# Thin V rows at the ends of the sequence, 128-column score weights, and other lengths in a planned kernel

## The chip, the cores and the metric

The kernel runs on one core of a Trainium2 chip. The metric is the device time of one execution in microseconds (us); the kernel before was timed three times, and the median counts. One further execution was taken with the hardware profiler, and all views of the profile are of that one.

## The reference

Two layers are applied, twice over in alternation: a segmented attention with a recurrent memory (A), and a gated feed-forward (B), each behind a layer normalisation and with a residual sum. Both applications use the same weights.

```python
x = x + A(layernorm(x))      # layer 0 attention
x = x + B(layernorm(x))
x = x + A(layernorm(x))      # layer 1 attention
x = x + B(layernorm(x))

def A(x):                    # x (1, 2048, 512); 32 heads of 128; 64 segments of 32 tokens
    mem = mem0               # 8 rows
    for s in range(64):
        h = concat([mem, x[segment s]])          # 40 rows
        q, k, v = h @ Wq, h @ Wk, h @ Wv         # per head
        p = softmax(mask(q @ k.T * scale))
        o = (p @ v) @ Wo
        mem = o[:8]; out[segment s] = o[8:]      # the memory goes to the next segment

def B(x):                    # F = 1792
    return (sigmoid(x @ w_gate) * (x @ w_up)) @ w_down
```

Data are bfloat16. The memory makes the 64 segments of a layer one after the other: no segment can begin its projections before the previous segment has finished its output projection.

## The kernel before

**Steps.** The kernel has 70 steps. In step t it works on segment t of layer 0 and on segment t - 6 of layer 1 (`LAG` = 6) together. So steps 0 to 5 hold layer 0 alone, steps 6 to 63 hold both layers, and steps 64 to 69 hold layer 1 alone. A tile hT (one of 8 in a ring) holds the normalised and transposed rows of one step in 80 columns: 32 tokens of layer 0, 8 memory rows of layer 0, 8 memory rows of layer 1, 32 tokens of layer 1. With one layer alone, 40 of the columns are used.

**Inside a step** (`emit_step`). The 32 heads go in five groups of six and one of two. For each group TensorE projects Q and K (L730, 8 matmuls of a head, weights of 128 columns from wq_sb and wk_sb, hT as the moving operand of 80 or 40 columns). ScalarE copies them to a tile qku, in which each head has 80 columns of Q followed by 80 of K. TensorE then makes the scores (L744), with the 80 columns of Q as the weights. VectorE adds the mask (L758) and does the softmax (L763 to L775) with the exponential on ScalarE (L768). TensorE transposes the probabilities (L787), and two copies bring them to ptsb. P·V follows (L808), with rows of V from a tile vsb as weights, then the output projection WO (L826), which adds up all heads in one bank. At the end the memory columns are copied to the next step's hT (L844 with one layer, L839 with two), which lets the next step begin.

**V comes in two ways.** V passes (`v_pass`, L584) take 128 token rows that were gathered in a tile (xvf or xvl) as weights, go over all 4096 columns of Wv in 32 matmuls of 512 columns, and write the result to a DRAM scratch tensor (scr). Each step reads its rows back into vsb (L685). A pass has 24 of every segment's 32 tokens. The other 8 tokens and the memory rows come from strips (`add_strips`, L698) inside the step: 32 columns of hT are the weights, four such matmuls stand side by side in the array, and 32 of them go over the 4096 columns. The result goes through a tile sst by DMA into vsb (L710).

**Which rows a pass holds.** A block is four segments (128 tokens), so 96 of its rows go through passes. For layer 0, three passes serve four blocks (`v_group`): blocks 0 to 5, 7, 8, 10, 11, 13, 14 are done this way ahead of the steps, in nine passes, of which the last (`late` = (10, 2)) is held back and planned with t = 4. Layer 1 has one pass for each block, once the block's feed-forward is done; it holds 96 rows of layer 1, and in twelve of the sixteen the other 32 rows are a third of block 6, 9, 12 or 15 of layer 0 (`v_fill`).

**Feed-forward** (`ffn`). After four segments a block has its feed-forward: two transposed products with 128 tokens moving (L926) and the down-projection (L950), with the weights streamed by GpSimd DMAs (L918, L919, L944). It uses xa for the residual sum, and the last sum of layer 1 goes to a tile xo and out. Its layer normalisations use small tiles lns, a power on GpSimd (L543) and transposes (L553).

**What sets the order.** All of this is described as tasks with a duration for each, their reads and writes, and buffers from pools. A planner (`Planner.plan`) walks through the tasks 24 times, forward and backward, with these durations, and keeps the order with the shortest span by its own account. The order on every engine and queue, and for some copies the engine too, is then fixed. So a changed duration changes the order of the whole program. Boot work carries a large `boost`: weights are loaded by SP in the order wv, then by group wq, wk and wo.

Of the kernel before, what the change touches and what calls it, by code (L numbers as in the profile page):

```python
# [16 lines left out]
P = 128  # L17
# [14 lines left out]
def mm_ns(n):  # L32
    return max(n / 2.4 + 2.3, 26.0)
# [323 lines left out]
class Kern:  # L357
# [40 lines left out]
    def setup_tiles(self):  # L398
# [10 lines left out]
        self.ident = c.tile([P, P], BF16, name="ident")  # L409
        self.maskb = c.tile([P, L], BF16, name="maskb")  # L410
        self.mask1 = c.tile([L, L], BF16, name="mask1")
        self.negh = c.tile([P, 1], F32, name="negh")
# [6 lines left out]
        self.mx = [c.tile([P, HG], F32, name=f"mx{i}") for i in range(3)]  # L419
# [5 lines left out]
        self.xo = [c.tile([P, D], BF16, name=f"xo{i}") for i in range(1)]  # L425
# [13 lines left out]
        self.lns = [c.tile([P, 12], F32, name=f"lns{i}") for i in range(3)]  # L439
# [21 lines left out]
    def clear(self):  # L461
# [3 lines left out]
        for k, t_ in enumerate(self.hT):  # L465
            pl.add("DVE", 120, lambda t_=t_: nc.vector.memset(t_[:, :, L:2 * L], 0.0), w=[("hT", k, 1, q) for q in ("m", "x")])
        for k, t_ in enumerate(self.pb):
            pl.add("DVE", 270, lambda t_=t_: nc.vector.memset(t_[:], 0.0), w=[("pb", k)])
        for k, t_ in enumerate(self.ptsb):
            pl.add("DVE", 320, lambda t_=t_: nc.vector.memset(t_[:], 0.0), w=[("ptsb", k, i) for i in (0, 1)])  # L470
        for k, t_ in enumerate(self.qku):
            pl.add("DVE", 320, lambda t_=t_: nc.vector.memset(t_[:], 0.0), w=[("qkz", k)])
        for k, t_ in enumerate(self.vsb):
            pl.add("DVE", 1130, lambda t_=t_: nc.vector.memset(t_[32:64], 0.0),
# [40 lines left out]
    def load_mem0(self):  # L515
        nc, pl, DC = self.nc, self.pl, self.DC
        m0 = self.xo[0][0:MEM, :]
        pl.add("SP", 100, lambda: nc.sync.dma_start(out=m0, in_=self.mem0), w=[("xo", 0)], lat=2500.0, boost=self.boot())
# [9 lines left out]
        pl.add("PE", 4 * 30, tr, r=[("xo", 0)], w=[B])  # L528
# [45 lines left out]
    def v_pass(self, tile, keys, pieces, boot=False):  # L574
# [3 lines left out]
        for k in range(self.H // 4):  # L578
# [15 lines left out]
            for c0, j, b, r0, n in pieces:  # L594
# [3 lines left out]
                pl.add(("SP", "POOL") if boot else "SP", {"SP": 450, "POOL": 760} if boot else 450,  # L598
# [4 lines left out]
    def v_group(self, blocks, psts, boot=False):  # L603

        cuts = [[(0, 0, 0, 24)], [(0, 96, 0, 8), (1, 0, 8, 16)], [(1, 64, 0, 16), (2, 0, 16, 8)], [(2, 32, 0, 24)]]
        base = self.cnt.get("xvf", 0)
        self.cnt["xvf"] = base + 3
        pcs = [[], [], []]
        for b, cut in zip(blocks, cuts):
            pst, B = psts[b] if b in psts else self.ln_x(b)  # L610
            for q, c0, r0, n in cut:
                xi = (base + q) % 2
                pcs[q].append((c0, 0, b, r0, n))
# [470 lines left out]
```

## Time and profile before

| what | value |
|---|---|
| median of 3 runs | 1827.25 us (1827.18 to 1829.39) |
| the profiled execution, its own time | 1827.17 us |
| its span in the trace | 1825.3 us |
| TensorE, busy | 1776.6 us |
| VectorE, ScalarE, GpSimd, busy | 1162.9, 1194.2, 569.9 us |
| moved by DMA | 272.11 MB |
| steps 0 to 5 end at | 78.4, 98.1, 116.8, 136.1, 156.2, 177.4 us |
| steps 63 to 68 end at | 1684.2, 1707.6, 1730.0, 1750.8, 1769.7, 1788.2 us |

The span is the time between the first and the last instruction of the program; the time of an execution has 1.9 us more around it. The ends of the steps are the starts of the memory copies L844 in the trace. In a group's row of the profile, the first number after the bar is the time in which at least one instruction of the group ran, and the second the mean duration of one. For TensorE a duration is not a cost: matmuls overlap in the pipeline, and what one costs is the distance between its start and that of the next. Weight loads (PEld) are rows of their own, and all of them are in the trace; of the matmuls some records are missing, so the loads serve for counting.

### The profile page before, as it was taken

What the parts mean: (1) busy time and instruction counts of PE and PEld (TensorE: products, weight loads), DVE (VectorE), ACT (ScalarE), POOL (GpSimd) and SP (SyncE); (2) the same over time, 40 slices, a digit from 0 to 9 for tenths busy, and PEclk for the clock granted to TensorE, in tenths of its full rate; (3) what the DMA queues carried; (4) which work ended last, traced back from release to release, by engine and by line L of the source; (5) the groups of instructions that cost most, each with busy time, mean ns of one, the idle gap of its engine ahead of it and who ended that gap; (6) DMA issues with size and microseconds to landing.
All of it is one profiled execution on the core that took longest, in us unless ns stands there. A gap on an engine that the chain in (4) does not pass through costs nothing.

```text
span 1825.3 us, 92117 instructions
## 1 busy us (share of the span) xinstructions
PE 1776.6 (97%) x39783; PEld 1533.6 (84%) x39970; DVE 1162.9 (64%) x3927; ACT 1194.2 (65%) x3005; POOL 569.9 (31%) x817
## 2 busy tenths in 40 slices
PE   7999999999999999999999999999999999999998
PEld 4678788988898888988898898888888898888886
DVE  5466655676666666666666667656666676656665
ACT  5666666676666666666666666666666666676664
POOL 5223032413233242413324141323324241333422
PEclk9999999999999999999999999999999999999999
DMA  9734254535445364535446363545536353544543
GB/s 351 233 108 148 62 155 121 163 100 176 147 153 157 103 204 122 170 109 169 149 124 187 109 194 100 170 131 155 158 110 196 117 168 95 173 144 127 174 124 107
DMA packets 138441, 272.11 MB, mean 149 GB/s; under 512 B 32954, under 2 KB 70594, under 8 KB 138034
## 3 DMA queue, kind: packets, MB, share of 16 engines
q0 software_dynamic: 56640, 183.09, 32.1%
q1 hardware_dynamic: 81394, 83.12, 15.4%
q8 instruction: 313, 5.13, 1.2%
q14 instruction: 94, 0.77, 0.1%
HBM read 221.85 MB, written 27.26 MB: 136 GB/s over the span
## 4 chain that ended last, share of the span: by engine, by line
PE 81%; DVE 9%; ACT 4%; SPq 3%; issue 2%; DMA 1%; POOLq 0%; ACTq 0%; DVEq 0%
PE bank L730 28%; PE bank L826 16%; PE bank L926 10%; PE bank L698 7%; PE bank L584 6%; PE bank L950 4%; PE bank L744 4%; PE bank L808 3%; DVE st L758 3%; SPq L485 3%; PE bank L787 2%; ACT ptsb L1024 1%; DVE pb L775 1%; DVE mx L763 1%; ACT qku L1024 1%
## 5 line engine op out<-in xcount | busy, mean ns | idle before, releaser
L730 PE MATMUL bank<-hT,wq_sb 128*128 128x80 bf16 (+1 forms) x8960 | 621.6, 198 | 3.5 <-issue 1.3
L730 PE MATMUL bank<-hT,wk_sb 128*128 128x80 bf16 (+1 forms) x8960 | 620.5, 198 | 3.2 <-DMA wk_sb<-in_A_Wk_dram 3.2
L1024 ACT CAST qku<-bank 128x480 bf16<-128x480 f32 (+3 forms) x770 | 391.1, 513 | 233.5 <-PE bank L730 165.7
L730 PEld LDWEIGHTS <-wq_sb 128*128 128x128 bf16 x8960 | 455.8, 99 | 38.5 <-issue 23.9
L730 PEld LDWEIGHTS <-wk_sb 128*128 128x128 bf16 x8960 | 450.6, 99 | 4.4 <-DMA wk_sb<-in_A_Wk_dram 3.6
L758 DVE TENSOR_TENSOR st<-bank,maskb 80x240 f32<-80x240 f32 (+1 forms) x732 | 267.9, 367 | 245.5 <-PE bank L744 238.7
L826 PE MATMUL bank<-otsb,wo_sb 128*128 128x80 bf16 (+1 forms) x8960 | 370.2, 198 | 9.6 <-ACT otsb L1024 8.1
L826 PEld LDWEIGHTS <-wo_sb 128*128 128x128 bf16 x8960 | 345.4, 99 | 35.0 <-issue 11.3
L918 POOL DMA_DIRECT2D wg<-in_B_w_gate_dram x217 | 164.7, 759 | 573.7 <-PE bank L926 520.2
L1024 ACT CAST otsb<-bank 128x480 bf16<-128x480 f32 (+3 forms) x420 | 199.9, 485 | 66.0 <-PE bank L808 51.7
L944 POOL DMA_DIRECT2D wd<-in_B_w_down_dram x217 | 154.2, 712 | 231.0 <-PE bank L744 88.7
L1024 ACT COPY ptsb<-bank 40x240 bf16<-40x240 bf16 (+3 forms) x546 | 170.8, 315 | 53.0 <-PE bank L787 46.0
L768 ACT ACTIVATE st<-st 80x240 f32<-80x240 f32 (+3 forms) x420 | 160.6, 383 | 45.8 <-DVE st L765 42.6
L770 DVE TENSOR_REDUCE mx<-st 80x6 f32<-80x240 f32 (+3 forms) x420 | 151.6, 364 | 50.7 <-ACT st L768 47.2
L926 PE MATMUL bank<-xnT,wg 128*128 128x128 bf16 (+2 forms) x1784 | 171.8, 218 | 2.0 <-issue 1.5
L926 PE MATMUL bank<-xnT,wu 128*128 128x128 bf16 (+2 forms) x1784 | 171.1, 218 | 0.0
L919 POOL DMA_DIRECT2D wu<-in_B_w_up_dram x217 | 162.7, 750 | 1.2 <-PE bank L926 0.5
L744 PE MATMUL bank<-qku 128*80 128x80 bf16 (+1 forms) x2240 | 160.2, 204 | 2.2 <-ACT qku L1024 1.6
L775 DVE TENSOR_TENSOR pb<-st,mx 80x240 bf16<-80x240 f32 (+3 forms) x420 | 154.9, 369 | 4.0
L765 DVE TENSOR_TENSOR st<-st,mx 80x240 f32<-80x240 f32 (+3 forms) x420 | 154.6, 368 | 4.2
L763 DVE TENSOR_REDUCE mx<-st 80x6 f32<-80x240 f32 (+3 forms) x420 | 153.0, 364 | 5.4
L543 POOL TENSOR_TENSOR lns<-lns,negh 128x1 f32<-128x1 f32 (+1 forms) x79 | 44.9, 570 | 357.0 <-DVE lns L542 319.7
(92 smaller groups left out, 2308.8 us busy)
## 6 DMA issues: line engine op xcount, KB each, us to landing
wg<-in_B_w_gate_dram POOLq DMA_DIRECT2D x220, 256.0 KB, 4.1
wu<-in_B_w_up_dram POOLq DMA_DIRECT2D x220, 256.0 KB, 4.5
wd<-in_B_w_down_dram POOLq DMA_DIRECT2D x220, 256.0 KB, 4.5
vsb<-scr SPq DMA_DIRECT2D x508, 48.0 KB
vsb<-sst SPq DMA_DIRECT2D x512, 32.0 KB
scr<-vst SPq DMA_DIRECT2D x136, 96.0 KB
wq_sb<-in_A_Wq_dram SPq DMA_DIRECT2D x10, 384.0 KB
wk_sb<-in_A_Wk_dram SPq DMA_DIRECT2D x10, 384.0 KB
```

The source lines that it names most:

```text
L730: nc.tensor.matmul(o_ap, lhsT=W[:, c, h * P:(h + 1) * P], rhs=mv(c), start=(c == 0), stop=(c == DC - 1))
L744: nc.tensor.matmul(s_all(SB)[full, w0 + i, :], lhsT=qku[:, i, 0, full], rhs=qku[:, i, 1, 0:ncol], start=True, stop=True)
L758: pl.add("DVE", dve_ns(n, True), lambda gsz=gsz, hs=hs, st=st, SB=SB, pj_=pj_, npj_=npj_, mk=mk, idx=idx: nc.vector.tensor_tensor(out=st[p ...
L763: pl.add("DVE", dve_ns(n), lambda hs=hs, st=st, mx=mx: nc.vector.tensor_reduce(out=mx[pr, hs], in_=st[pr, hs], axis=AX.X, op=ALU.max), r=s ...
L765: pl.add("DVE", dve_ns(n), lambda gsz=gsz, hs=hs, st=st, mx=mx: nc.vector.tensor_tensor(out=st[pr, hs], in0=st[pr, hs], in1=mx[pr, hs].uns ...
L768: pl.add("ACT", act_ns(n), lambda hs=hs, st=st: nc.scalar.activation(out=st[pr, hs], in_=st[pr, hs], func=ACTF.Exp, scale=self.scale), r=s ...
L775: nc.vector.tensor_tensor(out=pb[pr, hs, 0:L], in0=st[pr, hs], in1=rs[pr, 0:gsz].unsqueeze(2).to_broadcast([npart, gsz, L]), op=ALU.mult)
L826: nc.tensor.matmul(WB[:, c * ncol:(c + 1) * ncol], lhsT=self.wo[:, h, c * P:(c + 1) * P], rhs=otsb[:, hl, 0:ncol], start=(h == 0 and c == ...
L918: pl.add("POOL", 760, lambda wg=wg, fs=fs: nc.gpsimd.dma_start(out=wg[:], in_=self.wgv[:, :, fs]), r=[("wo", self.H - 1)], w=[gk] + bt, la ...
L919: pl.add("POOL", 760, lambda wu=wu, fs=fs: nc.gpsimd.dma_start(out=wu[:], in_=self.wuv[:, :, fs]), r=[("wo", self.H - 1)], w=[uk] + bt, la ...
L926: nc.tensor.matmul(gu[:, 2 * i + k, 0:n], lhsT=W[:, c, i * P:(i + 1) * P], rhs=xnT[:, c, rw], start=(c == 0), stop=(c == DC - 1))
L1024: nc.scalar.copy(out=dst, in_=src)
```

## The change

1. *Thin steps.* In steps 0 to 3 and 66 to 69 (`thin`), the strips take 32 token and memory rows: 24 tokens and the memory, for 8 tokens and 16 memory rows before. The columns are `MEM` to `MEM + 32` of hT in the first four steps, `L` to `L + 32` in the last four. The scratch tensor must hold only the other 8 rows of each such segment, and the step reads only those.
2. *Passes.* Block 0 therefore needs 8 of its 24 rows per segment in a pass. `v_group` takes its cuts as an argument and is called with blocks (0, 1), (2, 14), (3, 4, 5, 7) and (8, 10, 11, 13): eight passes ahead of the steps, and none held back. Block 14 gives 8 rows per segment there; its other 16, and block 15, are filled into the passes of layer 1 (`fills`), so that block 14 is loaded and normalised twice. Block 15 of layer 1 has no pass: a strip set of 32 rows (`strips`) goes by sst straight to the scratch tensor in four DMAs.
3. *Score weights.* The weights of a score matmul are 128 columns of qku in place of 80: 80 of Q and the first 48 of K. The result has 128 rows, of which the softmax reads as many as before.
4. *Lengths.* In the planner, reads of V are 375 for 430, strip DMAs 600 for 430, writes of passes 380 (whole rows) or 650 for 450, and a strip set 130 less. Strips of steps with layer 0 now name both layers' columns of hT as read.
5. *Boot.* The fills with zero of hT, pb, ptsb, qku and vsb go from VectorE to GpSimd.
6. *Tiles.* ident, maskb, mask1 and negh become parts of a tile cst, lns and mx parts of a tile small. The tile xo is gone: the last sum is written in place of xa, and mem0 is loaded to a part of hff.

The diff, cut to its core:

```diff
-        self.ident = c.tile([P, P], BF16, name="ident")
...
+        cst = c.tile([P, P + 2 * L + 8], BF16, name="cst")
+        self.ident, self.maskb, self.mask1 = cst[:, 0:P], cst[:, P:P + L], cst[0:L, P + L:P + 2 * L]
+        self.negh = cst[:, P + 2 * L:P + 2 * L + 2].bitcast(F32)
+        small = c.tile([P, 48], F32, name="small")
...
-        self.xo = [c.tile([P, D], BF16, name=f"xo{i}") for i in range(1)]
...
-            pl.add("DVE", 320, lambda t_=t_: nc.vector.memset(t_[:], 0.0), w=[("qkz", k)])
+            pl.add("POOL", 500, lambda t_=t_: nc.gpsimd.memset(t_[:], 0.0), w=[("qkz", k)])
...
-                pl.add(("SP", "POOL") if boot else "SP", {"SP": 450, "POOL": 760} if boot else 450,
+                pl.add(("SP", "POOL") if boot else "SP", {"SP": 450, "POOL": 760} if boot else (380 if n == XS else 650),
...
+    def strips(self, cols, keys):
+        nc, pl, DC = self.nc, self.pl, self.DC
+        vb = [pl.buf(self.bank), pl.buf(self.bank)]
+        def mm():
+            for q in range(2):
+                for c in range(DC):
+                    for i in range(4):
+                        k = 2 * i + q
+                        nc.tensor.matmul(vb[q][32 * i:32 * i + 32, :], lhsT=cols(c), rhs=self.wv[:, c, k * 512:(k + 1) * 512],
+                                         start=(c == 0), stop=(c == DC - 1), skip_group_check=True)
+        sb = pl.buf(self.sstp)
+        pl.add("PE", 2 * DC * (mm_ns(512) + 12) + 20, mm, r=keys + [("wv", h) for h in range(self.H)], w=vb, use=[sb])
...
+        alone = not both and t - j0 * LAG in self.thin[j0]
+        skeys = [("hT", slot, j, k) for j in (0, 1) for k in ("m", "x")] if j0 == 0 else hkeys
...
+            lo, nx = (2 * 8 * j, 8) if alone else (0, XS)
...
-                        nc.tensor.matmul(s_all(SB)[full, w0 + i, :], lhsT=qku[:, i, 0, full], rhs=qku[:, i, 1, 0:ncol],
+                        nc.tensor.matmul(s_all(SB)[:, w0 + i, :], lhsT=fview(qku[:, i, 0, 0:1], [(1, P)]), rhs=qku[:, i, 1, 0:ncol],
...
-            if g == 0:
+            if g == 0 and alone:
+                add_strips(L if j0 else MEM, [(j0, 0, 0 if j0 else MEM, 32, "vs")])
+            elif g == 0:
                 add_strips(SCOL, [(0, 0, SCOL, 16, "vs"), (1, 16, 0, 16, "vs")])
...
-            oi = self.nxt("xo", len(self.xo))
-            xo, ok = self.xo[oi], ("xo", oi)
+            xo, ok = xa, ("xa", xi)
...
+            if b == self.NBLK - 1:
+                self.take_v(pst2, B2, 1, self.xvl[q], [("xvl", q, 0)], 0, 16, 8)
+                self.write_hT_x(pst2, B2, 1, BLK * b + self.LAG)
+                sb = self.strips(lambda c: self.xvl[q][:, c, 0:32], [("xvl", q, 0)])
...
+                return
...
-        self.late = (10, 2)
+        self.thin = (range(BLK), range(self.NSEG - BLK, self.NSEG))
+        fills = {0: (6, ((0, 0), (1, 8), (2, 16))), 3: (9, ((3, 0), (4, 8), (5, 16))), 6: (12, ((6, 0), (7, 8), (8, 16))),
+                 9: (14, ((9, 8), (10, 16))), 11: (15, ((11, 0), (12, 8), (13, 16)))}
...
-        self.v_group([0, 1, 2, 3], {0: p0, 1: p1}, True)
-        self.v_group([4, 5, 7, 8], {}, True)
-        self.v_group([10, 11, 13, 14], {}, True)
+        cuts = [[(0, 0, 0, 24)], [(0, 96, 0, 8), (1, 0, 8, 16)], [(1, 64, 0, 16), (2, 0, 16, 8)], [(2, 32, 0, 24)]]
+        self.v_group([0, 1], {0: p0, 1: p1}, [[(0, 96, 0, 8)], [(0, 0, 0, 24)]])
+        self.v_group([2, 14], {}, [[(0, 0, 0, 24)], [(0, 96, 0, 8)]])
+        self.v_group([3, 4, 5, 7], {}, cuts)
+        self.v_group([8, 10, 11, 13], {}, cuts)
...
-            if t == 4:
-                tile, keys, pieces = self.held
-                self.v_pass(tile, keys + [("hT", (t + 1) % self.R, 0, "m")], pieces)
```

The lines of the changed kernel are numbered a little differently: V passes are L583, strips L660, projections L734, scores L748.

## The prediction

> **What bounds the kernel now.** I read the page first: its busy line and its slices.
>
> ```profile
> PE 1776.6 (97%) x39783; PEld 1533.6 (84%) x39970; DVE 1162.9 (64%) x3927; ACT 1194.2 (65%) x3005; POOL 569.9 (31%) x817
> ...
> PE  7999999999999999999999999999999999999998
> ...
> DMA  9734254535445364535446363545536353544543
> ...
> PE 81%; DVE 9%; ACT 4%; SPq 3%; issue 2%; DMA 1%; POOLq 0%; ACTq 0%; DVEq 0%
> ```
>
> TensorE is full in every slice but the first and the last, and holds 81% of the chain that ended last (fourth line); DMA is high only in the first two slices. A busy PE is not yet a PE at its pace, so I took the spacing of matmuls from the timeline (columns: start us, us, engine, line, ...): the start of the next row minus the start of this one, over the count.
>
> ```profile
> 86.48 0.25 PE L730 MATMUL bank<-hT,wk_sb 128*128 128x40 bf16 x4
> 86.58 0.38 PE L744 MATMUL bank<-qku 128*80 128x40 bf16 x6
> 86.81 0.26 PE L730 MATMUL bank<-hT,wq_sb 128*128 128x40 bf16 x4
> ...
> 81.49 1.91 PE L698 MATMUL bank<-wv_sb,hT 128*32 128x512 bf16 x32
> 83.33 0.29 PE L744 MATMUL bank<-qku 128*80 128x40 bf16 x3
> ...
> 90.02 1.89 PE L584 MATMUL bank<-wv_sb,xvf 128*128 128x512 bf16 x8
> 91.75 0.46 PE L826 MATMUL bank<-otsb,wo_sb 128*128 128x40 bf16 x12
> ```
>
> So a projection matmul of 40 columns costs 0.10/4 = 25 ns, a score matmul of 40 columns 0.23/6 = 38 ns, a strip matmul 1.84/32 = 57.5 ns (a whole strip set 1.84 us), a V-pass matmul 1.73/8 = 216 ns (a pass of 32: 6.9 us). In the two-layer steps, at 80 columns, the same reading gives 35.8 ns for projections (704.80 to 706.23 us, 40 of them) and 38.3 for scores (0.23/6, rows at 712.00 and 713.95). Pricing every weight load of the trace at its spacing (the loads are complete; some matmul records are missing) gives 1752 us of PE work in a span of 1825.3: about 10 us of the 73 idle lie before 28 us, 5 more before 69 us, where the stream of weights is waited for, and 10 to 13 in the last six steps.
>
> Then I cut the span at the copies that carry the memory to the next step (L844, L839). Stretches, with columns PE, PEld, DVE, ACT, POOL, clock, DMA:
>
> ```profile
> 116.80:136.00 19.20, 17.30 (x492) 15.18 (x491) 14.14 (x52) 12.40 (x43) 8.28 (x12) 0.91 0.48 152
> 156.20:177.40 21.20, 20.98 (x550) 17.63 (x552) 14.62 (x51) 14.10 (x45) 10.09 (x14) 1.00 0.64 197
> 205.10:229.20 24.10, 23.64 (x514) 19.86 (x517) 13.98 (x50) 16.31 (x39) 0.00 (x0) 1.00 0.24 66
> 1707.60:1730.00 22.40, 21.65 (x533) 17.28 (x536) 14.76 (x49) 14.72 (x47) 7.15 (x10) 1.00 0.45 136
> 1769.70:1788.20 18.50, 16.65 (x503) 14.53 (x502) 12.68 (x43) 11.23 (x38) 5.16 (x7) 1.00 0.42 124
> ```
>
> A one-layer step owns 256 x 25 + 32 x 38 + 32 x 36 (transposes and P·V) + 128 x 25 ns + 1.84 us = 13.8 us of PE; what else it holds is filler (V passes, feed-forward). The last row (step 68) holds 15.8 us of work and takes 18.5; the first (step 3) holds 14.5 and takes 19.2, 1.7 of which are the clock of 0.91. There the softmax chain on DVE sets the length: **a floor of about 18.3 us**. The other rows hold 21 to 23 us of work each: PE-bound, and shorter work shortens them. Two-layer steps average 26.0 us (104 per four) with some 0.6 of idle each.
>
> **What the skill says.** The Trainium skill, *TensorE: Matmul & The Clock Gate*, section "Weight-path perf modes — Fast Weight Load (FWL) and DoubleRow": fast loading is on when there are 128 weight columns and the type is not FP32. The trace agrees: loads of 128 columns (L730) take 99 ns, those of 80 (L744) 121, and the matmuls behind them are spaced 25 against 38. Its section "Back-to-back issue gap" gives N/2.4 + 2.5 ns with a floor of about 25: 216, 36 and 25 here, as measured. *Perfetto Trace Analysis*, "Identifying the Most-Contended Engine", wants weight-load share rather than matmul busy: 84%. *VectorE: DVE Perf Modes*, "Zero memsets can be issued as uint32 (trn2)", says that DVE zeroes 4 bytes per element; the trace shows it (240 uint32 in 0.26 us), and the change gives that up by moving the fills to POOL.
>
> **The change, part by part.**
>
> *V rows.* Before, 800 weight loads stand on L584 (512 from xvl, 288 from xvf): 25 passes. After, the built program has 736 and one more strip set. Gone are 64 x 216 ns = 13.8 us, added 1.84. The pass held back to t = 4 (blocks 10, 11, 13, 14) runs before in 156–177 us (8 loads), 205–229 (19) and the rest soon after: -6.9. The layer-1 pass of block 15 runs in 1707–1730 (23) and 1730–1751 (9): -6.9 + 1.84 = -5.1. Block 14 is normalised twice: 4 transposes, +0.2 on PE; its DVE (1.4 us) and POOL (0.6) lie beside PE work, since DVE is 64% and POOL 31% busy; on a full DVE they would cost themselves.
>
> *Score weights.* All 2,240 score loads become 128 columns. 1,856 of 80 columns go from 38.3 to 35.8: 4.6 us. 384 of 40 columns go from 38 to 25: 5.0. The rows written beyond 80 are read by nobody.
>
> PE work thus falls by 12.0 - 0.2 + 9.6 = 21.4 us. **How much comes through:**
> - Held pass: of 6.9, step 5 gets 1.7 (21.2 to 19.5 before its scores, above the floor). In the built order step 7 drops from 22.9 to 19.4 us of work; DVE alone is 14 us there, with some 4 before its first score and 2.5 after its last, so about 21 is least. I take 1.0 off: 5.9.
> - Block 15: steps 65 to 68 get 18.5, 17.3, 16.5 and 16.0 us of work; with the floor and 0.9 of idle their lengths become 19.5, 18.4, 18.3, 18.3 for 22.4, 20.8, 18.9, 18.5 — 6.1, of which 1.5 is the scores': 4.6. Its chain is not longer: a strip set for a pass, 4 issues to DRAM for 8, on the same SP queue (scr and vsb issues take 0.4 to 0.6 us each; the queue is not full).
> - Scores, two-layer: all 4.6. One-layer: half, 2.5; steps 0, 2, 3, 68, 69 sit on the floor or on DMA.
> - Transposes: -0.2.
>
> *Shorter reads of V, and 32 strip rows.* In eight steps 8 rows are read for 24, the strip DMAs carry 32 rows for 16: the issues are as many. Boot passes are 8 as before. Cover: in the boot, weights on DMA until 69 us; at the end, PE. Nothing.
>
> *Fills on POOL.* 128 bf16 elements take 0.20 us there, 40 take 0.13: 0.8 ns each, so 480 take 0.5, 384 0.4, 2048 1.7. Ahead of the first power (L543, at 6.63 us before) stand one hT, three qku, three pb and one vsb fill: 4.7 us after 2.1, done by about 7. DVE is freed of 7 us. Cost 0 to 1 at the first pass, behind which POOL's other powers and scr issues queue; the weights' arrival covers it until 69 us. I take 0.5.
>
> *xo gone, small tiles merged.* The last sum is written in place of xa, used again two feed-forwards (some 50 us) later. The built program's waits on POOL and DVE are of the same kinds and numbers: no new one. Nothing. If an output landed late, DVE would wait with the next sum, and PE behind it.
>
> *Lengths in the plan.* The planner now books 0.60 for a strip DMA, 0.375 for a read and 1.84 for a strip set; the trace has 0.62, 0.38 and 1.84. The whole order is new. PE's order in one period of four steps differs, but the work between a product and its consumer is alike (projection to score at least about 1 us, softmax 5 us); only the cover of the memory copy is thinner in some steps (0.45 us for 0.9). No view prices this: from -0.1 to +0.25 us per step, that is -6 to +15 over 58 steps. I take 0 for the sum and keep both ends.
>
> Sum: 5.9 + 4.6 + 4.6 + 2.5 - 0.2 - 0.5 = **16.9 us**. The profiled execution took 1827.17 us (span 1825.3 and 1.9 around it), 0.1 below the median of 1827.25, so no correction: **1810.3**.
>
> **Rivals.**
> 1. *Only the full stretches pay.* One-layer steps are all at the floor, and the tail gains nothing: 5.9 + 4.6 - 0.5 = 10 us, 1817. For: steps 3 and 68. Against: steps 5, 65, 66 with 21 to 22 us.
> 2. *The fast load doesn't come*, since the 128 columns are 80 of q and 48 of k: 7.1 less, 1817. Against: they are contiguous, and L730 shows it.
> 3. *Slower: the new order starves PE in two-layer steps*, at its place where a step's first projections follow WO with 0.45 us of cover, and where feed-forward's second half follows closely on the first. It decides from 0.36 us per step (21 over 58 steps); at 0.45, +26 - 17: 1836. For: in the built program 102 of those loads wait on DVE, for 52 before. Against: the same planner leaves 0.6 now, and now with lengths that are nearer the trace.
> 4. *A better order*: 0.1 us less per step and the tail in full: 1801.
>
> **Numbers.** 0.2% (3.7 us) is about what a measurement of this kernel can tell from no change. Forecast 0.56, rivals 1 and 2 together 0.20 (all three faster), 4 0.10, 3 0.14; of the last, the weak third ends within 0.2%. Faster 0.85, same 0.05, slower 0.10. The range 1800 to 1823 leaves out most of rival 3 and a little of 4.
>
> **What would show it.** Right: 736 loads on L583; score loads near 99 ns and spaced 25 and 36; step 65 near 19.5 us; steps 64 to 69 shorter by 6 to 7 in all; PE work near 1731. Wrong: two-layer steps above 104 us per four; step 7 or 65 as long as before; score loads still at 121 ns; the first V pass after 10.6 us.

## The result and the profile after

| | before | after |
|---|---|---|
| median, beside each other on one chip | 1827.22 us (1826.72 to 1829.39, 4 runs) | 1826.09 us (1825.04 to 1830.10, 4 runs) |
| ratio | | 0.9996, 95% interval 0.9978 to 1.0013 |
| again, in a later run | 1827.55 us (35 runs) | 1826.73 us (12 runs), ratio 0.9992, 0.9983 to 1.0001 |

No difference that can be told: the forecast of 1810.3 us missed, and the time lies above its range (1800 to 1823). The profiled execution of the changed kernel took 1830.1 us, so its trace holds 4 us that the median does not have. A second profile of it (e2_same, below) took 1830.1 us too, so what one of the two traces shows alone is not put down to the kernel.

The page of the changed kernel, in the lines that answer to those of before, with the line of TensorE's granted clock added:

```profile
PE 1763.5 (96%) x39743; PEld 1522.8 (83%) x39942; DVE 1178.3 (64%) x3933; ACT 1175.2 (64%) x2969; POOL 580.2 (32%) x838
...
PE   7999999999999999999999999999999999999998
...
PEclk9989999999999999999999999999999999999999
DMA  9734252636455364635446364545546453554543
...
PE 85%; ACT 5%; DVE 3%; SPq 3%; issue 2%; DMA 1%; POOL 0%; ACTq 0%; POOLq 0%; DVEq 0%
```

TensorE is busy for 13 us less in a span that is 3 us longer. The third slice of the clock has fallen to 8. The weight loads by line and shape (time in the union, mean ns of one, then the idle time before them and its releasers) say that the work did go:

```profile
L748 PEld LDWEIGHTS <-qku 128*128 128x128 bf16 x2240 | 111.0, 99 | 25.7 <-ACT sst L1039 9.3 <-ACT qku L1039 2.5 <-issue 0.6
L583 PEld LDWEIGHTS <-xvl 128*128 128x128 bf16 x480 | 40.7, 98 | 34.4 <-issue 1.3 <-ACT xvl L1039 0.2
L583 PEld LDWEIGHTS <-xvf 128*128 128x128 bf16 x256 | 23.1, 98 | 24.8 <-issue 2.9 <-DVE xvf L1041 0.3
```

There are 736 loads of V passes for 800, and all 2,240 score loads take 99 ns for 121. In the timeline the scores of 40 columns are now spaced 25 to 26 ns and those of 80 are spaced 35 to 37.

The same five steps as in the prediction (length, then busy time of PE, PEld, DVE, ACT, POOL, clock, DMA share, GB/s):

```profile
116.00:137.50 21.50, 17.99 (x493) 15.81 (x493) 14.70 (x55) 11.99 (x40) 8.31 (x12) 0.77 0.49 141
158.70:179.70 21.00, 18.72 (x538) 16.28 (x539) 13.49 (x46) 12.63 (x43) 9.00 (x13) 1.00 0.59 174
208.90:232.40 23.50, 20.90 (x502) 18.61 (x504) 12.88 (x46) 16.70 (x42) 0.00 (x0) 1.00 0.19 51
1710.80:1734.80 24.00, 20.60 (x546) 16.33 (x545) 13.80 (x50) 13.94 (x44) 7.17 (x10) 0.93 0.37 109
1771.50:1789.70 18.20, 16.48 (x500) 14.24 (x501) 11.67 (x41) 11.18 (x37) 4.31 (x6) 1.00 0.43 125
```

Steps 5 and 7 lost 2.3 and 2.7 us of busy TensorE, but only 0.2 and 0.6 us of length. Step 3 and step 65 are longer than before (19.2 and 22.4), both with a lower clock. In the second profile step 3 is as long (21.5 us), but step 65 takes 21.4 us at full clock, with the same two waits in it as in the first (1.2 us for pb, 1.0 for otsb):

```profile
1713.20:1734.70 21.50, 19.04 (x550) 15.67 (x548) 13.77 (x50) 13.98 (x44) 7.15 (x10) 1.00 0.41 121
```

So some 2.5 of its 24.0 us belong to that one execution.

To follow this through all kernels I price every weight load of a program at the spacing of the matmul behind it, step by step, and call the rest of a step's length its idle time. The prices are those of the prediction, with 56 ns for 128 columns moving, 42 for 96 and 25 for 32. This idle time holds waits as well as time lost to a low clock. Its level depends on the prices, the differences between kernels by about 1 us. "Half clock" is the time at a clock of 0.5, without the last few us.

| profiled execution | work | idle in steps 0 | 1–5 | 6–11 | 12–57 | 58–63 | 64–69 | idle, all | half clock |
|---|---|---|---|---|---|---|---|---|---|
| before | 1742.0 | 15.4 | 7.9 | 7.2 | 32.2 | 4.8 | 15.7 | 83.3 | 6.8 |
| after | 1720.6 | 15.9 | 14.7 | 12.5 | 33.8 | 8.1 | 22.7 | 107.7 | 20.5 |
| after, second profile | 1720.6 | 17.1 | 14.3 | 14.0 | 35.2 | 6.8 | 20.4 | 107.7 | 20.5 |

The work fell by 21.4 us, as forecast. That is counts times prices, so it confirms the counts and the spacings and nothing more. The idle time rose by 24.4. Of this rise only 1.6 us (3.0 in the second profile) lie in the 46 full steps of two layers; the rest lies in the steps ahead of them and behind them. The clock can account for at most some 7 us: half of the 13.7 us by which its low stretches grew, an estimate that takes every matmul in them for twice as long.

**One place of it, step 3.** The rows show start and length; the idle time before a row is in brackets.

```profile
121.63 2.42 SPq L714 DMA_DIRECT2D vsb<-sst  x4
121.67 0.75 POOL L925 DMA_DIRECT2D wu<-in_B_w_up_dram  x1
122.41 2.11 POOL L950 DMA_DIRECT2D wd<-in_B_w_down_dram  x3
...
125.73 0.28 PE L791 MATMUL bank<-cst,pb 80*128 80x80 bf16 x3
128.33 0.36 PE L814 MATMUL bank<-ptsb,vsb 104*128 104x80 bf16 x3 [2.32 <-issue]
```

The four strip DMAs now carry 32 rows each, and they are issued in the middle of the first nine feed-forward weight loads (117.9 to 124.5 us, 2.36 MB). P·V needs vsb and begins 2.3 us late. The view names no releaser for this wait; in e2_oldlens, below, it names one for the same wait there, the DMA from sst to vsb (1.6 us). Before, with 16 rows, the same P·V began at 127.61 us and had waited 0.3 us for ptsb. From 127.6 us on the clock stands at half for 13.7 us.

### The profile page after: what moved, and what is told of

Same layout as the page of the kernel before. It is cut to its first block, busy times and chain, and to the rows that moved or that the text cites. A ratio compares the mean times of both kernels' runs of the same rounds, so it can differ in the third digit from the quotient of the medians.

```text
span 1828.3 us, 91963 instructions
## 1 busy us (share of the span) xinstructions
PE 1763.5 (96%) x39743; PEld 1522.8 (83%) x39942; DVE 1178.3 (64%) x3933; ACT 1175.2 (64%) x2969; POOL 580.2 (32%) x838
## 4 chain that ended last, share of the span: by engine, by line
PE 85%; ACT 5%; DVE 3%; SPq 3%; issue 2%; DMA 1%; POOL 0%; ACTq 0%; POOLq 0%; DVEq 0%
PE bank L734 31%; PE bank L832 17%; PE bank L932 9%; PE bank L660 7%; PE bank L583 6%; PE bank L956 4%; PE bank L748 4%; PE bank L814 3%; SPq L484 3%; PE bank L791 2%; ACT qku L1039 1%; ACT ptsb L1039 1%; ACT otsb L1039 1%; DVE st L762 1%; PE bank L552 1%
## 5 line engine op out<-in xcount | busy, mean ns | idle before, releaser
L734 PE MATMUL bank<-hT,wq_sb 128*128 128x80 bf16 (+1 forms) x8960 | 622.3, 198 | 9.0 <-issue 5.0
L734 PE MATMUL bank<-hT,wk_sb 128*128 128x80 bf16 (+1 forms) x8960 | 621.5, 198 | 2.8 <-DMA wk_sb<-in_A_Wk_dram 2.5
L734 PEld LDWEIGHTS <-wq_sb 128*128 128x128 bf16 x8960 | 454.8, 99 | 37.7 <-issue 27.5
L734 PEld LDWEIGHTS <-wk_sb 128*128 128x128 bf16 x8960 | 450.5, 99 | 5.0 <-DMA wk_sb<-in_A_Wk_dram 3.0
L762 DVE TENSOR_TENSOR st<-bank,cst 40x240 f32<-40x240 f32 (+3 forms) x768 | 279.5, 368 | 225.0 <-PE bank L748 216.0
L1039 ACT CAST otsb<-bank 128x480 bf16<-128x480 f32 (+3 forms) x420 | 196.2, 486 | 72.8 <-PE bank L814 55.1
L1039 ACT COPY ptsb<-bank 40x240 bf16<-40x240 bf16 (+2 forms) x552 | 173.9, 316 | 40.5 <-PE bank L791 32.2
L774 DVE TENSOR_REDUCE small<-st 80x6 f32<-80x240 f32 (+3 forms) x420 | 151.8, 364 | 46.6 <-ACT st L772 43.6
L769 DVE TENSOR_TENSOR st<-st,small 80x240 f32<-80x240 f32 (+3 forms) x420 | 154.1, 369 | 4.0
L767 DVE TENSOR_REDUCE small<-st 80x6 f32<-80x240 f32 (+3 forms) x420 | 152.7, 365 | 5.5
L748 PE MATMUL bank<-qku 128*128 128x80 bf16 (+1 forms) x2240 | 154.3, 198 | 1.6 <-issue 0.5
L779 DVE TENSOR_TENSOR pb<-st,small 80x240 bf16<-80x240 f32 (+3 forms) x420 | 152.7, 369 | 4.5
L542 POOL TENSOR_TENSOR small<-small,cst 128x1 f32<-128x1 f32 (+1 forms) x80 | 44.4, 557 | 348.3 <-DVE small L541 345.3
```

The costliest lines, as they stand in the source:

```text
L734: nc.tensor.matmul(o_ap, lhsT=W[:, c, h * P:(h + 1) * P], rhs=mv(c), start=(c == 0), stop=(c == DC - 1))
L748: nc.tensor.matmul(s_all(SB)[:, w0 + i, :], lhsT=fview(qku[:, i, 0, 0:1], [(1, P)]), rhs=qku[:, i, 1, 0:ncol], start=True, stop=True)
L762: pl.add("DVE", dve_ns(n, True), lambda gsz=gsz, hs=hs, st=st, SB=SB, pj_=pj_, npj_=npj_, mk=mk, idx=idx: nc.vector.tensor_tensor(out=st[p ...
L767: pl.add("DVE", dve_ns(n), lambda hs=hs, st=st, mx=mx: nc.vector.tensor_reduce(out=mx[pr, hs], in_=st[pr, hs], axis=AX.X, op=ALU.max), r=s ...
L769: pl.add("DVE", dve_ns(n), lambda gsz=gsz, hs=hs, st=st, mx=mx: nc.vector.tensor_tensor(out=st[pr, hs], in0=st[pr, hs], in1=mx[pr, hs].uns ...
L1039: nc.scalar.copy(out=dst, in_=src)
```

## The experiments

Each expectation was written before its run. The theory at the start (A): TensorE bounds the steps, so that removed work comes through. Against it (B): a floor in the step, set by the softmax chain. Then: strips against weights (1), VectorE's part of the chain (2), and the new order (3). Times are medians; ratios are to the kernel before on the same chip. Differences in us are worked out from the ratios, since the kernels ran on several chips, unless the text says that they are of medians. The edits are shown in short.

### One removed piece at a time, in the order of before

Here nothing is planned again: every engine keeps the order of the kernel before.

```diff
# e1_scores: 128 columns of score weights
-lhsT=qku[:, i, 0, full]
+lhsT=fview(qku[:, i, 0, 0:1], [(1, P)])
# e1_held, e1_last: the held pass, or the pass of block 15
-for c in range(DC):
+for c in range(1):
```

> The kernel before in its own order, with one edit: the score weights are 128 columns of qku. Work removed from TensorE, in program order times spacing: 1,856 x 2.5 ns with 80 columns moving and 384 x 13 ns with 40, 9.6 us in all. Theory A (each step is bounded by TensorE, so what its work loses its length loses): 1818 to 1820. Theory B (in steps of two layers the softmax on VectorE and ScalarE sets a floor near 23.5 us; only the steps that hold a pass lie above it): the 3.6 us of steps 12 to 57 come through, of the 5.0 us of the one-layer steps half or less: 1821 to 1824. If the faster load is worth nothing in the order before: 1826 to 1828.

Measured: 1821.49 us, ratio 0.9964 (0.9951 to 0.9977), that is -6.6 us. The forecast for this piece was 7.1. In its trace, steps 0 to 11 are 1.0 us shorter in all, steps 12 to 57 2.5, steps 58 to 63 0.4, and steps 64 to 68 1.8. So the two-layer steps gave 3.2 us where 4.6 were forecast (an estimate from one trace of each), and the one-layer steps the 2.5 that were forecast. This part of the prediction holds.

> The kernel before in its own order; of the held pass (planned with t = 4, spread over steps 5 to 11) only 8 of the 32 matmuls run, so that the rows of V which it makes are incomplete: 24 x 216 ns = 5.2 us of TensorE work less. Theory A (TensorE bounds these steps): -4.4 us, as forecast in proportion (5.9 of 6.9): about 1822.8. Theory B (the softmax floor of about 23.5 us holds in steps 6 to 11 and the pass had filled waits): -0.5 to -2: 1825 to 1826.7.

Measured: 1827.68 us, ratio 0.9997 (0.9988 to 1.0005). Worth nothing. Step 7 of before, and then steps 5 and 7 of this kernel:

```profile
205.50:229.60 24.10, 23.64 (x515) 19.85 (x517) 13.98 (x50) 16.29 (x38) 0.00 (x0) 1.00 0.25 64
```

```profile
156.30:177.60 21.30, 20.43 (x548) 17.20 (x546) 14.67 (x52) 13.98 (x45) 10.09 (x14) 1.00 0.64 193
205.60:229.70 24.10, 21.91 (x506) 18.65 (x505) 14.02 (x51) 16.32 (x39) 0.00 (x0) 1.00 0.22 62
```

Step 7 lost 3.1 us of work (22.9 to 19.8 by the prices; it held 20 matmuls of the pass and holds 5) and no length, at full clock. Before, its only wait of note was one of 0.28 us; now there are four:

```profile
219.77 0.38 PE L808 MATMUL bank<-ptsb,vsb 104*128 104x80 bf16 x6 [0.33 <-ACT ptsb L1024]
221.29 1.02 PE L826 MATMUL bank<-otsb,wo_sb 128*128 128x80 bf16 x24 [0.92 <-ACT otsb L1024]
224.75 0.28 PE L787 MATMUL bank<-ident,pb 80*128 80x80 bf16 x3 [0.35 <-DVE pb L775]
225.45 0.38 PE L808 MATMUL bank<-ptsb,vsb 104*128 104x80 bf16 x6 [0.41 <-ACT ptsb L1024]
```

The pass had stood in the waits between scores, probabilities and output. Without it TensorE waits there for the copies. In this order the step had been at its floor already, although it looked 98% busy.

> The kernel before in its own order; of the layer-1 pass of block 15 (in steps 65 to 68) only 8 of the 32 matmuls run, so that its rows of V are incomplete: 5.2 us of TensorE work less. Theory A: all of it comes off: 1822. Theory B (one-layer steps have a floor near 18 us and idle grows in them): -3 to -4, since steps 65 and 66 (22.4 and 20.9 us) are well above that floor: 1823 to 1824. If the tail is bound by something other than TensorE (as the changed kernel's step 65 of 24.0 us would say): -1 or less, 1826 and more.

Measured: 1825.40 us, ratio 0.9994 (0.9986 to 1.0003): -1.1 us with an interval that takes in nothing. Step 65 went from 22.4 to 21.8 us for 3.5 us less of work, and step 66 from 20.9 to 19.4 for 1.7 less, with waits for pb, ptsb and otsb in the place of the pass. The profiled execution was the fastest of the twelve; the others took up to 6 us more, at a granted clock down to 0.995 for its 0.999.

> The kernel before in its own order with all three edits (128-column score weights, a quarter of the held pass, a quarter of block 15's layer-1 pass; V rows of those two passes incomplete): 20 us of TensorE work less, as much as the whole change takes away (20.5), without new order, lengths or strips of 32 rows. Theory A: -17 to -19, about 1809. Theory B: -8 to -11, about 1817, the rest lost to the floors. Then the changed kernel's other 7 to 9 us would have been lost to its strips and its order. If -2 or less, the order and the strips are not to blame at all and the work removed was never on the path.

Measured: 1820.30 us, ratio 0.9960 (0.9946 to 0.9974): -7.3 us of 20. Theory B, and a little below it. The three pieces make 6.6 + 0.5 + 1.1 = 8.2 alone. In its trace 17.1 us are at half clock, for 6.8 before: at most 5 of the 13.6 us by which idle time rose.

So the work removed is worth 7 us in the old order. The changed kernel shows none of it. What else it changes has to have cost as much: the strips, the fills at the start, or the order.

### The changed kernel again, and its weights later

> The changed kernel once more, unchanged, for a second profile and times on this chip. If the half-clock stretch of 13.7 us from 127.6 us on belongs to the kernel, it is there again, with the 2.3 us wait of P.V in step 3 ahead of it, and the time is 1826. If it was an accident of the first profile, which took 4 us more than the other runs, it is missing, and the loss must be looked for elsewhere.

Measured: the second line of the first table. The trace repeats the first one: P·V of step 3 waits 2.34 us, and the clock is low for 13.7 us from 129.2 us on. The stretch belongs to the kernel. The 2.5 us of step 65 do not.

```diff
# e2_latew: in the finished order, the nine first loads behind the next entry of GpSimd
+mv = [tk for tk in order if tk in self.moved]
+at = order.index(mv[-1])
+nx = next(i for i in range(at + 1, len(order)) if order[i].on == "POOL")
+order = [tk for tk in order[:nx + 1] if tk not in mv] + mv + order[nx + 1:]
```

> The changed kernel; order unchanged on every engine but GpSimd's queue: the nine first feed-forward weight loads (issued from 117.9 us) stand behind the power of the layer normalisation that follows them, so they are issued after the strips' DMAs of step 3 have landed. Theory 1 (the strips' DMAs share the DMA engines with the 2.36 MB of weights; P.V of step 3 waits 2.32 us; TensorE's clock then drops to half for 13.7 us): step 3 falls from 21.5 to 18.5 us, no long half-clock stretch near 130 us, and 4 to 7 us go: 1819 to 1822 against the changed kernel's 1826. Rival (the drop of the clock comes anyway, from the order of steps 3 and 4): no stretch is moved, within 1 us of 1826. Rival (the weights come late for the feed-forward and are missed there): step 4 to 6 longer, 1826 or more.

Measured: 1825.22 us, ratio 0.9988 (0.9982 to 0.9995). Steps 3 and 4 of this kernel:

```profile
115.90:135.50 19.60, 17.05 (x493) 14.78 (x493) 14.75 (x55) 11.99 (x40) 8.34 (x12) 0.91 0.53 153
135.50:154.90 19.40, 19.38 (x559) 17.25 (x560) 14.08 (x49) 12.49 (x41) 7.53 (x11) 1.00 0.43 122
```

Step 3 falls from 21.5 to 19.6 us, step 4 from 21.4 to 19.5, and 3.4 us are left of the low stretch; P·V now waits 1.0 us, for ptsb. The loads begin only 2.6 us later (120.5 us for 117.9), and two of the nine are still ahead of the strips' DMAs. The other traces agree. With 16 rows, as before, the longest wait of P·V in step 3 is 0.4 to 1.1 us, although the strips fall among the loads there too (six traces). With 32 rows and five or six loads ahead it is 1.1 to 2.8 us and the step takes 20.4 to 21.7 us (eleven traces); with 32 rows and two or fewer ahead, 0.3 to 1.0 us and 18.8 to 19.6 (three traces). So both are needed, and theory 1 names the mechanism of that place rightly. Its size is another matter: the medians differ by 1.5 us and the ratios by 0.7, not by 4 to 7, and the two intervals overlap. In this trace the clock fell in four other places (174.9, 1721, 1752 and 1800 us).

### What sets the floor of step 7

```diff
# e2_nomax: both left out
-nc.vector.tensor_reduce(out=mx[pr, hs], in_=st[pr, hs], axis=AX.X, op=ALU.max)
-nc.vector.tensor_tensor(
-    out=st[pr, hs], in0=st[pr, hs], in1=mx[pr, hs].unsqueeze(2).to_broadcast([npart, gsz, L]), op=ALU.subtract)
# e3_otsb: after planning, the copies of P·V in steps 3 to 11 and from 58; e5_nomax_otsb: both edits
+tk.on = "DVE"        # was ACT
```

> The changed kernel in its own order, without the maximum over each row and its subtraction in the softmax: two of VectorE's operations in each group less, and the chain from scores to P.V shorter by them. Theory 2 (this chain sets the floor of a step once the passes are gone): steps 6 to 11 and 58 to 63 fall towards their TensorE work (7: from 23.5 to about 21, 65 by 1 to 2), steps 12 to 57, which are full of work, hardly move, and one-layer steps lose up to 1 us each: 1805 to 1815. Rival (TensorE's work and the spacing of its instructions set the steps; VectorE's waits are not what ends last): within 2 us of 1826.

Measured: 1823.14 us, ratio 0.9977 (0.9966 to 0.9987), some 3 us below the changed kernel. But step 7 says that theory 2 is wrong:

```profile
208.10:231.60 23.50, 20.89 (x503) 18.55 (x504) 10.06 (x33) 16.75 (x42) 0.00 (x0) 1.00 0.19 51
```

VectorE has 2.8 us less to do and the step is as long as it was (23.5 us). The waits before scores, P·V and output projection are the same ones, 0.2 to 0.5 us each, for ScalarE's copies otsb, ptsb and qku. In the last steps it is the same. Steps 66 to 68 together, of the changed kernel and of this one:

```profile
1734.80:1789.70 54.90, 51.98 (x1569) 46.06 (x1574) 37.91 (x136) 34.24 (x110) 15.96 (x22) 1.00 0.43 125
```

```profile
1728.20:1783.20 55.00, 52.52 (x1574) 46.04 (x1574) 28.44 (x100) 34.27 (x111) 15.96 (x22) 1.00 0.44 125
```

They had been forecast at 55.0 us, with the softmax chain on VectorE as the floor. The number came, but with 9.5 us less for VectorE the length is the same: its load is not the floor of one-layer steps either.

> The changed kernel in its own order; in steps 3 to 11 and from 58 on the copies of P.V to otsb (six of 0.56 us in a step of two layers) run on VectorE in place of ScalarE. In step 7 (23.5 us long for 19.4 us of TensorE work) the waits name ScalarE's copies, and leaving out two of VectorE's operations moved that step by nothing. If ScalarE's queue sets the floor there: steps 7 and 10 fall by 1 to 2 us each, steps 65 to 68 by some tenths, the whole by 3 to 6: 1821 to 1824. If the chain from score to output projection is just that long, whichever engine copies: step 7 stays within 0.3 us and the whole within 1.5 of 1826.7. If VectorE's softmax stands ahead of the copies: longer, 1828 and more.

Measured: 1848.34 us, ratio 1.0114 (1.0098 to 1.0129). Much slower, the third case of the expectation: otsb is copied behind the softmax.

> The changed kernel in its own order, without the maximum and its subtraction in the softmax, and with the copies to otsb on VectorE in steps 3 to 11 and from 58 on. Each edit alone left step 7 at 23.5 us (the first) or made it 26.4 (the second, where the copies stood behind the softmax). Both together take 3 us from ScalarE and leave VectorE with no more than before. If the two queues set the floor: step 7 at 22 to 22.5 us and the whole at 1818 to 1821. If the length of the chain from score to output projection sets it: step 7 still within 0.4 us of 23.5, the whole at 1822 to 1825. If VectorE's copies still come late: step 7 above 24 and the whole above 1826.

Measured: 1832.49 us, ratio 1.0025 (1.0014 to 1.0037): again the third case, above 1826. Step 7 of e3_otsb and of this kernel:

```profile
208.10:234.50 26.40, 23.60 (x502) 21.30 (x504) 16.02 (x52) 13.95 (x36) 0.00 (x0) 0.87 0.17 45
```

```profile
209.50:235.50 26.00, 23.57 (x503) 21.26 (x504) 13.34 (x39) 14.15 (x36) 0.00 (x0) 0.87 0.17 45
```

ScalarE has 2.6 us less to do, and the step is 2.5 us longer; each holds 6.8 us at half clock, which cost at most 3.4. By this estimate the steps would be 23.0 and 22.6 us long without them. So VectorE's load is not what sets the floor, and moving these copies away from ScalarE did not lower it by much either. What remains is the succession itself: score, copy, softmax, transposition, copy, P·V, copy, output, with TensorE coming back to each link in the order that the planner fixed. I did not test that link by link, so it stays argued. In all orders tried step 7 took between 22.4 and 26.4 us, for 18.7 to 23.7 us of work.

### The lengths in the plan

```diff
# e2_oldlens: the changed kernel with the lengths of before (e3_blens: the reverse)
-reads 375, strip DMAs 600, writes 380 or 650, a strip set + 20
+reads 430, strip DMAs 430, writes 450,        a strip set + 150
```

> The changed kernel planned again with the old lengths (reads, strips and writes of V 430, 430 and 450, a strip set 130 longer), so with another order everywhere. Rival 3 (the new lengths make an order that costs what the work saves): about 1810, as forecast. Theory (strips against weights, the clock and the floors cost, not the lengths): 1820 to 1832, whichever way the new order happens to fall, and again a stretch of half clock in steps 3 to 5 if strips and weights meet there.

Measured: 1819.62 us, ratio 0.9957 (0.9941 to 0.9974). That is just below what the theory allowed, and far above the rival's 1810: the lengths cost something, but not as much as the work saves.

> The kernel before, planned again with the new lengths alone (its work as it was: reads of V 375, strips 600, writes 380 or 650, a strip set 130 less). The changed kernel with the old lengths took 1819.6, with the new ones 1826.7. If the new lengths themselves make a worse order: 1833 to 1836 here. If any new plan is a draw (each length gives another order, and orders of like span by the planner's account differ by several us on the chip): anywhere within 1820 to 1836, without a reason in the lengths.

Measured: 1834.36 us, ratio 1.0037 (1.0023 to 1.0052). This is what was expected of the lengths, but it lies within the range of the draw as well. The four together:

| | old lengths | new lengths |
|---|---|---|
| work of before | 1 | 1.0037 (+6.8 us) |
| work of after | 0.9957 (-7.9 us) | 0.9992 (-1.5 us) |

Read by columns, the change of work is worth -7.9 or -8.3 us; read by rows, the new lengths cost 6.8 or 6.4. (The strips that name both layers' columns as read go with the work here.) That is the account of the result: **some 8 us gained, some 7 given back by the order**. Each of the four entries is one planned order, so this is what these orders cost, and not yet what a length costs. From e2_oldlens to the changed kernel (to its second profile in brackets) the steps 1 to 5 grew by 2.9 (2.4) us, 6 to 11 by 2.9 (4.4), 58 to 63 by 5.4 (4.0) and 64 to 69 by 4.3 (2.0), while 12 to 57 became 3.1 (1.7) shorter. So the order took its cost at both ends of the program. The next six kernels ask which length it is, and whether any other order would do the same.

```diff
# e3_lens2: the new lengths, shifted by 10        # e5_old2: the old ones, shifted by 10
+reads 385, strip DMAs 590, writes 390 or 640, a strip set + 30
+reads 440, strip DMAs 440, writes 440,        a strip set + 140
# the old lengths with one of the new: e4_strip, e4_set, e4_write, e4_read
+strip DMAs 600
+a strip set + 20
+writes 380 or 650
+reads 375
```

> The changed kernel, planned again with lengths 10 away from its own (390 and 640 for 380 and 650, 385 for 375, 590 for 600, a strip set 10 longer), so with the same account of the hardware but another order. If the lengths matter as such, they are as good as the same: 1825 to 1828. If an order is a draw, it differs from 1826.7 by several us in either direction, and the steps that change are those with little work to fill them (3 to 11 and 58 to 68), not 12 to 57.

Measured: 1824.86 us, ratio 0.9983 (0.9976 to 0.9991).

> The changed kernel with the old lengths shifted by 10 (440 for 450, 440 for 430, a strip set 140 longer), so nearly the same account and another order. If the old lengths give a better order for a reason: 1818 to 1822. If an order is a draw with a spread as wide as the 7 us in dispute: anything from 1816 to 1830.

Measured: 1819.75 us, ratio 0.9963 (0.9951 to 0.9976). A shift of 10 moves the time by 2 us at most, near either set of lengths, though it gives another order. That speaks against a pure draw, but the shifted sets are only 3.7 us apart (5.1 in the medians), for 6.4 unshifted.

> The changed kernel with the old lengths but for one: the DMAs from sst to vsb keep 600. With all the old lengths it took 1819.6, with all the new ones 1826.7. If this length carries the cost (a step's strips seem later to the planner, so work is put ahead of P.V that then pushes the chain back): 1825 to 1828. If not: 1818 to 1821. In between: the order is a draw.

Measured: **1810.82 us, ratio 0.9906 (0.9891 to 0.9922)**.

> The changed kernel with the old lengths but for one: a strip set of TensorE keeps the shorter length (130 less). If this length carries the cost: 1825 to 1828; if not: 1818 to 1821.

Measured: 1821.83 us, ratio 0.9967 (0.9955 to 0.9978).

> The changed kernel with the old lengths but for the writes to the scratch tensor, which keep 380 for whole rows and 650 for others and for the strip set of block 15. If these carry the cost: 1825 to 1828; if not: 1818 to 1821.

Measured: 1833.39 us, ratio 1.0033 (1.0018 to 1.0049).

> The changed kernel with the old lengths but for the reads of V rows, which keep 375 for 430. If this length carries the cost: 1825 to 1828; if not: 1818 to 1821.

Measured: 1816.64 us, ratio 0.9930 (0.9906 to 0.9954).

Against the old lengths (0.9957), the new length of the writes costs 13.9 us, that of the strip DMAs brings 9.3, that of the reads 4.9 (its interval overlaps that of the old lengths), and that of a strip set costs 1.8. These four effects add to 1.5 us, all four at once make 6.4. So they do not simply add, and three of the four runs fell outside both of their expected ranges. The writes' length is the one that costs beside the old others; the new lengths with the old writes were not run, so it is not shown that it carries the cost in the changed kernel. One and the same work took 1810.8 to 1833.4 us in eight orders.

Where the two extremes part is in the full steps, against my expectation: steps 12 to 57, of before, after, e4_strip and e4_write:

```profile
335.80:1531.70 1195.90, 1180.21 (x26265) 1039.51 (x26379) 778.83 (x2616) 794.18 (x1951) 384.91 (x535) 1.00 0.49 148
```

```profile
336.80:1530.80 1194.00, 1175.27 (x26261) 1037.00 (x26395) 798.06 (x2643) 784.99 (x1936) 387.27 (x539) 1.00 0.52 149
```

```profile
333.90:1517.70 1183.80, 1176.62 (x26378) 1033.33 (x26377) 788.43 (x2641) 789.37 (x1931) 386.24 (x537) 1.00 0.53 150
```

```profile
337.00:1543.10 1206.10, 1187.75 (x26412) 1038.53 (x26409) 787.68 (x2645) 788.01 (x1933) 388.21 (x541) 1.00 0.52 148
```

By the prices the work there is 1163.6, 1160.2, 1158.8 and 1161.0 us, the idle time 32.2, 33.8, 25.0 and 45.2. TensorE's waits of note in that window, for e4_strip and then e4_write (us in total, times, longest):

```profile
PE bank L832 <- ACT otsb L1039: 3.7, 17, 0.3
PE bank L660 <- DVE hT L845: 1.7, 5, 0.4
```

```profile
PE bank L832 <- ACT otsb L1039: 8.1, 27, 0.6
PE bank L748 <- ACT qku L1039: 2.1, 5, 0.4
PE bank L814 <- DMA vsb<-sst: 1.9, 4, 0.8
```

In the poor order TensorE comes to the output projection before otsb more often (27 times for 17), and four times to P·V before its strips. Of the 20.2 us of idle time between the two, 12.8 lie in four steps, 22, 30, 42 and 50. In e4_write each takes 27.3 or 28.3 us for 23.3 of work, where e4_strip idles 0.1 to 1.3 us. Step 30 of e4_write:

```profile
809.40:836.70 27.30, 25.25 (x543) 21.12 (x542) 15.42 (x55) 18.76 (x44) 1.09 (x2) 1.00 0.22 63
```

Step 15 of the same kernel does 23.6 us of work in 24.3, so such a step need not be long. Step 6 of e4_write, 35.4 us long for 28.6 with the old lengths, shows how an order does that elsewhere. SP's queue, with e2_oldlens first:

```profile
180.53 13.53 SPq L714 DMA_DIRECT2D vsb<-sst  x12
```

```profile
189.04 5.93 SPq L714 DMA_DIRECT2D vsb<-sst  x8
195.07 3.62 SPq L1035 DMA_DIRECT2D scr<-vst  x6
198.80 0.40 SPq L703 DMA_DIRECT2D vsb<-scr  x1
199.29 3.10 SPq L714 DMA_DIRECT2D vsb<-sst  x4
...
202.36 0.73 PE L814 MATMUL bank<-ptsb,vsb 104*128 104x80 bf16 x16 [1.12 <-DMA vsb<-sst]
```

The strip set itself stands 8.3 us later in the step (9.6 us after its start for 1.3), its DMAs follow, and four of them come behind six writes; P·V waits, and the clock falls twice. Why longer writes make the planner choose this was not tried.

### The edits together

The diffs of e2_oldlens, e2_latew and e2_nomax, in one kernel.

> The changed kernel with the old lengths, the first nine feed-forward weight loads one GpSimd power later, and the softmax without its maximum and subtraction: the three edits that lowered the time one by one (by 7.1, 1.5 and 3.6 us). If they add up: 1814 to 1815. If the order that the old lengths give has already lost the waits that the other two remove: 1817 to 1819.

Measured: 1812.15 us, ratio 0.9921 (0.9904 to 0.9938), 6.6 us below e2_oldlens (7.5 in the medians). The three edits add up, and a little more: 1814 to 1815 was expected. The changed kernel with 600 for the strip DMAs and the old lengths otherwise (e4_strip) is as good and computes the softmax as the reference does; it is the best version found, 17 us below the kernel before. In it step 65 takes 19.8 us. It still has the wait of step 3: P·V waits 2.3 us there, and the step takes 21.7 us.

## Why the prediction was wrong

1. **The work**: right. 736 loads, 99 ns, 25 and 36 ns, and 21.4 us less by the prices. The level was off: with the prices that the prediction gives, the loads of the kernel before make 1742 us and not 1752, so it was idle for 83 us and not 73, with 16 us in the last six steps for 10 to 13.
2. **The scores, 4.6 + 2.5 us**: right. Alone they brought 6.6 (4.2 to 9.0).
3. **The held pass, 5.9 us**: the first failed term. In proportion e1_held should have brought 4.4; its best value is 0.5, and 2.2 at the end of its interval. I took the least length of step 7 as "about 21", from VectorE's 14 us of work. In that order the step stayed at 24.1 us with 3.1 us less work, in the changed kernel it took 23.5, and it isn't VectorE's load that sets it. The fault was to take a high busy share for a bound: the pass filled waits. Step 5, counted for 1.7 us, kept its 21.3.
4. **The pass of block 15, 4.6 us**: failed in size in the old order (1.1 measured for 3.5 in proportion). In the changed kernel step 65 took 24.0 us in one profile and 21.4 in the other, for 19.5 forecast, with the same two waits; steps 66 to 68 came as forecast (54.9 us for 55.0), but not for the reason given, as e2_nomax shows. In e4_strip step 65 takes 19.8 us and in e3_best 20.0. So the forecast length is nearly reached where an order allows for it, and the new one did not.
5. **The lengths, taken as 0 between -6 and +15**: the second failed term. They cost 6.4 to 6.8 us, inside the ends. I had priced them per two-layer step over 58 steps; in the changed kernel the loss lay in steps 1 to 11 and 58 to 69. The lengths of writes, which alone cost 13.9 us beside the old others, were not in my list at all; I had compared only strips, reads and the strip set with the trace.
6. **"Shorter reads of V, and 32 strip rows", nothing**: the cover was named wrongly. In step 3 there is neither boot traffic nor spare time: the strips' DMAs lie under the first feed-forward weights, and P·V waits 2.3 us. By e2_latew this is worth 1.5 us in the medians and 0.7 by the ratios, with intervals that overlap.
7. **Fills on POOL, 0.5 us**: about right in size. The first power comes at 6.6 us, as before. The first pass starts at 10.98 us for 9.55, past the 10.6 that was named as a sign of being wrong, but step 0 ends only 0.3 us later. VectorE is freed of under 6 us, not 7.
8. **Idle time as a constant**: under all of these. I subtracted work and kept the idle. In e1_all3 idle rose by 13.6 us when 20.0 of work were taken away.

Of the rivals, the number of the first, "only the full stretches pay" (1817), lies near what the work is worth by itself (1820), but partly by luck: the held pass, on which it rests, paid next to nothing. The second is refuted (99 ns; 25 and 36). The third, TensorE starved in two-layer steps by a new order, did not come in this kernel (1194.0 us for 1195.9 in steps 12 to 57), but it did in e4_write, and its opposite, the fourth, in e4_strip.

## What to carry to other kernels

Before work is counted as saved, ask what the engine would do in its place: if what comes next is still waiting for a copy at that point, the work was filling a wait, and a step that looks 98% busy can give nothing back. Where an order is planned from durations, compare the changed work in several orders (here the same work took 1810.8 to 1833.4 us) before the change is judged, and keep an old order for reference. A duration that is nearer the trace need not give a better order.

## What the runs showed of the hardware

TensorE's clock falls to half in pieces of 3.4 us or multiples of it (3.4, 6.8, 10.2, 13.7 us), as the Trainium skill, *TensorE: Matmul & The Clock Gate*, section "What's actually happening", has it with its window of 3413 ns. That section has the fall after at least one idle window. Here, in the 20 traces, none of the 65 falls had a whole idle window ahead of it: in the 3.4 us before a fall TensorE was idle for 0.7 to 2.9 us, in several waits or one, and no single wait in the 7 us before was longer than 2.9 us. A wait of 2.3 us with thin work behind it came before 13.7 us at half clock, and in e3_otsb waits of 0.25, 0.70 and 0.48 us came before 6.8 us of it in step 7. The sums at half clock are 6.8 us in the kernel before, 17.1 with the three pieces taken out of its order, and 10.2 to 23.9 in the eight orders of the changed kernel's work. So a new wait may cost more than its own length; that it did so here is argued from these sums and not shown by a run. Nor does the clock tell the good orders from the poor ones: the fastest, e4_strip, has 17.1 us at half clock.
